# Three passes for VectorE's exp in place of five, and eighteen more score banks moved there from ScalarE

## The chip, the cores and the metric

One core of a Trainium2 chip. The metric is the device time of one execution in microseconds (us); lower is better. These kernels run on one core, so a slow state can only be told from other runs of the same kernel; all timed runs quoted here are of the state fast, and single looks (rounds 0) are of state unknown and said to be so. A ratio is taken over fast runs of the same rounds, so it is not quite the ratio of the medians quoted beside it.

## The reference

A layer normalization, 16-head attention over 2048 tokens (head size 28), and an MLP with GELU whose SiLU gates the attention's result.

```python
def _A_ref(x, wqkv, wo):                      # x: (1, 2048, 448), already normalized
    ...                                       # q, k, v: 16 heads of 28
    scores = jnp.einsum("bhqd,bhkd->bhqk", q, k) * Dh ** -0.5
    p = _softmax(scores, axis=-1)
    o = jnp.einsum("bhqk,bhkd->bhqd", p, v)
    return (...o...) @ wo

s = _A_ref(xn, A_wqkv, A_wo)
g = _silu(_B_ref(xn, B_w1, B_b1, B_w2, B_b2))  # B: GELU MLP, 448 -> 1792 -> 448
return x + s * g
```

The scores are 1024 tiles of 128 keys by 512 queries, each one PSUM bank. Every element of them needs an exp: that is the bulk of ScalarE's work.

## The kernel before

The kernel is a Python list scheduler. It holds a duration for every instruction, decides the order of each engine's instructions in advance, and emits semaphore waits for the dependencies. On the chip each engine then works down its own fixed list.

Scores are made three banks at a time (a *unit*), in a ring of six PSUM banks. ScalarE takes one exponential over the unit's banks. For some units the last bank is given to VectorE (a *late* bank), and ScalarE's exponential covers two. VectorE first evicts the bank to SBUF, which frees it, and works the exp out later, for two such banks at a time where it can.

```python
# eviction of a late bank: fixed point, the exponent's bits above bit 16
eng.tensor_scalar(K.ysb[i][...], K.ring[:, RB[m], :], SM_SCALE * LOG2E * 65536.0,
                  127.0 * 65536.0, op0=ALU.mult, op1=ALU.add)        # int32 out
...
# p_exp2: five passes over 512 or 1024 columns; lo is the low half of y as uint16
v = lo * (EXP_SC / 65536)          # tensor_scalar
u = (v + EXP_A) * v                # scalar_tensor_tensor
u = (u + EXP_B) * u                # scalar_tensor_tensor
u = v * EXP_D + u                  # scalar_tensor_tensor
pl = y * 2**-9 + u                 # scalar_tensor_tensor, written as uint16 = the bits of a bf16
```

Which units give a bank away is decided while the schedule is made: `pick_late` compares VectorE's backlog with a threshold `THS` for the block (one block is 64 banks) and with what is left of the block plus `SLACKS`. The product with V needs all of a block's late banks before the block's accumulator can be evicted. When PE's recent load is low, the scheduler also has it issue small products on zeros (L881). This is filler that changes no result.

## Time and profile before

| | before |
|---|---|
| time, median of 3 | 483.54 us (483.23 to 483.59) |
| span of the profiled run | 481.2 us |
| busy: ScalarE / PE / VectorE | 470.0 / 438.9 / 406.4 us |
| exponentials on ScalarE | 350 for 948 banks; 76 banks on VectorE |

To read it: ScalarE is the engine without gaps, so the question for each part of a change is what it does to ScalarE's list of exponentials, and whether something makes that list wait. The lines are in the prediction.

### The profile page before, as it was taken

Reading aid. Unit: us, or ns where it says so; the run is one execution under the profiler, and the core shown is the slowest. Engines: PE = TensorE matmul, PEld = TensorE weight load, DVE = VectorE, ACT = ScalarE, POOL = GpSimd, SP = SyncE. Lnnn points to the kernel's source line nnn. Section 1 sums busy time; section 2 is a strip of 40 time slices with the busy share of each in tenths; the row PEclk is TensorE's granted clock in tenths of the full one; section 3 lists DMA queues with packets and bytes.
Section 4 is the critical chain, followed back from the end, with each engine's and each line's share of the span. In section 5 each row is a group of like instructions: output and inputs, shape, how many; then the busy total and the mean of one; then the engine's idle time right before and its main releaser. Section 6 shows DMA issues by size and latency. Waiting matters only on the chain.

```text
span 481.2 us, 10207 instructions
## 1 busy us (share of the span) xinstructions
PE 438.9 (91%) x4256; PEld 169.1 (35%) x4293; DVE 406.4 (84%) x607; ACT 470.0 (98%) x394; POOL 44.7 (9%) x77
## 2 busy tenths in 40 slices
PE   6999899999988988999989988999999999899995
PEld 4443333333332333323223443333333333333453
DVE  8947789889988899999898759888897899889885
ACT  6999999999999999999999999999999999999994
POOL 7470000000000101010101000010100101000001
PEclk9999999999999999999999999999999999999998
DMA  8301000000000000000400000000101001011011
GB/s 262 136 11 26 1 1 1 1 2 2 1 1 0 1 1 1 2 2 0 135 1 0 1 2 1 0 2 1 40 0 40 2 1 38 1 59 59 3 41 40
DMA packets 8288, 11.10 MB, mean 23 GB/s; under 512 B 1649, under 2 KB 6897, under 8 KB 8242
## 3 DMA queue, kind: packets, MB, share of 16 engines
q1 hardware_dynamic: 7954, 9.75, 6.5%
q8 instruction: 34, 0.56, 0.5%
q10 hardware_dynamic: 288, 0.69, 0.4%
q14 instruction: 12, 0.10, 0.1%
HBM read 8.61 MB, written 1.84 MB: 22 GB/s over the span
## 4 chain that ended last, share of the span: by engine, by line
ACT 49%; PE 30%; issue 16%; DVE 4%; DMA 1%; POOL 0%; ACTq 0%; DVEq 0%
ACT P L1192 45%; PE ring L1153 9%; PE acc L1378 5%; PE misc L1089 4%; ACT h L1068 3%; PE misc L1031 2%; PE misc L719 2%; PE acc L881 2%; PE misc L973 1%; DVE st L629 1%; PE ring L1031 1%; DMA x_sb<-in_A_x_dram 1%; PE ring L719 1%; PE misc L1474 0%; PE ring L973 0%
## 5 line engine op out<-in xcount | busy, mean ns | idle before, releaser
L1192 ACT ACTIVATE P<-ring 128x1536 bf16<-128x1536 f32 (+1 forms) x350 | 428.8, 1501 | 0.7 <-PE ring L1153 0.5
L1153 PE MATMUL ring<-qT,kT 32*128 32x512 bf16 (+2 forms) x1144 | 136.7, 359 | 23.7 <-ACT P L1192 19.0
L1378 PE MATMUL acc<-P,vaug 128*32 128x512 bf16 (+2 forms) x1074 | 94.9, 362 | 0.5 <-issue 0.5
L1153 PEld LDWEIGHTS ring<-qT,kT 32*128 32x128 bf16 x1144 | 35.8, 91 | 130.6 <-ACT P L1192 122.2
L1215 DVE TENSOR_SCALAR x_sb<-ring 128x512 int32<-128x512 f32 x68 | 46.8, 688 | 17.7 <-PE ring L1153 16.5
L1089 PE MATMUL misc<-w,h 128*128 128x448 bf16 x224 | 51.4, 355 | 0.3
L1447 POOL CAST rhi<-rc 128x16 bf16<-128x16 f32 x15 | 11.8, 790 | 399.0 <-DVE rc L1445 296.3
L881 PE MATMUL acc<-ident,zero 128*128 128x128 bf16 x543 | 47.7, 221 | 0.2 <-issue 0.2
L1378 PEld LDWEIGHTS acc<-P,vaug 128*32 128x32 bf16 x1074 | 24.4, 93 | 51.2 <-issue 44.9
L881 PEld LDWEIGHTS acc<-ident,zero 128*128 128x128 bf16 x543 | 31.5, 98 | 21.9 <-issue 20.0
L1031 PE MATMUL misc<-xnT,w 128*128 128x512 bf16 x127 | 36.1, 382 | 1.8 <-issue 1.3
L1336 DVE SCALAR_TENSOR_TENSOR x_sb<-x_sb,kT 128x1024 uint16<-128x1024 int32 (+1 forms) x25 | 26.8, 1070 | 0.5
L1334 DVE SCALAR_TENSOR_TENSOR kT<-kT 128x1024 f32<-128x1024 f32 (+1 forms) x25 | 26.8, 1071 | 0.4
L1014 DVE CAST h<-misc 128x512 bf16<-128x512 f32 x35 | 24.0, 685 | 3.8 <-PE misc L1031 3.5
L1330 DVE SCALAR_TENSOR_TENSOR kT<-kT 128x1024 f32<-128x1024 f32 (+1 forms) x25 | 26.7, 1068 | 0.5
L1332 DVE SCALAR_TENSOR_TENSOR kT<-kT 128x1024 f32<-128x1024 f32 (+1 forms) x25 | 26.7, 1067 | 0.3
L1089 PEld LDWEIGHTS misc<-w,h 128*128 128x128 bf16 x224 | 17.7, 97 | 23.1 <-issue 10.7
L1031 PE MATMUL ring<-xnT,w 128*128 128x512 bf16 x82 | 19.4, 380 | 1.7 <-ACT h L1068 1.6
L1334 DVE SCALAR_TENSOR_TENSOR w<-w 128x1024 f32<-128x1024 f32 (+1 forms) x20 | 20.6, 1032 | 0.3
L1332 DVE SCALAR_TENSOR_TENSOR w<-w 128x1024 f32<-128x1024 f32 (+1 forms) x20 | 20.6, 1030 | 0.2
L1336 DVE SCALAR_TENSOR_TENSOR x_sb<-x_sb,w 128x1024 uint16<-128x1024 int32 (+1 forms) x20 | 20.6, 1031 | 0.2
L1330 DVE SCALAR_TENSOR_TENSOR w<-w 128x1024 f32<-128x1024 f32 (+1 forms) x20 | 20.5, 1026 | 0.3
(160 smaller groups left out, 447.4 us busy)
## 6 DMA issues: line engine op xcount, KB each, us to landing
h<-in_A_x_dram SPq DMA_DIRECT2D x4, 448.0 KB, 3.2
w<-in_B_w_dram SPq DMA_DIRECT2D x1, 1568.0 KB, 8.4
w<-in_B_w_dram SPq DMA_DIRECT2D x1, 1344.0 KB, 8.6
out_dram<-h SPq DMA_DIRECT2D x6, 224.0 KB, 1.9
x_sb<-in_A_x_dram SPq DMA_DIRECT2D x2, 448.0 KB, 4.9
h<-in_A_wqkv_dram SPq DMA_DIRECT2D x3, 168.0 KB, 5.1
x_sb<-in_A_x_dram ACTq DMA_DIRECT2D x1, 448.0 KB, 4.7
out_dram<-h SPq DMA_DIRECT2D x4, 112.0 KB, 1.7
```

The lines of the kernel that those rows point to most:

```text
L881: ins = eng.matmul(K.acc[:, 0:128], K.zero[:, :], K.ident[:, :], start=False, stop=True, skip_group_check=True)
L1014: yield _Task(DVE, lambda eng: eng.tensor_copy(dst, bank), [tok], wr, 0.69, 0.0, 2)
L1031: ins = eng.matmul(bank, K.w1[:, kt, ft * 128:(ft + 1) * 128], K.xnT[:, kt, c * 512:(c + 1) * 512], start=(kt == 0), stop=(kt == KT - 1))
L1089: ins = eng.matmul(ps, hv[:, ft, t * 128:(t + 1) * 128], K.w2[:, ft, :], start=(ft == 0), stop=(ft == FT - 1))
L1153: return eng.matmul(K.ring[:, RB[m], col:col + nq], K.kT[32 * j:32 * j + 32, g, t * 128:(t + 1) * 128], K.qT[32 * j:32 * j + 32, g, c * 51 ...
L1192: return eng.activation(K.P[:, p0:p0 + n, :], K.ring[:, b0:b0 + n, :], ACTF.Exp, scale=SM_SCALE)
L1215: yield _Task(DVE, lambda eng, m=m, i=i, half=half: eng.tensor_scalar(K.ysb[i][:, 512 * half:512 * half + 512], K.ring[:, RB[m], :], SM_SC ...
L1330: yield _Task(DVE, lambda eng: eng.scalar_tensor_tensor(u, v, EXP_A, v, op0=ALU.add, op1=ALU.mult), [tv], [tu], d1, 0.0, 4)
L1332: yield _Task(DVE, lambda eng: eng.scalar_tensor_tensor(u, u, EXP_B, u, op0=ALU.add, op1=ALU.mult), [tu], [tu], d1, 0.0, 4)
L1334: yield _Task(DVE, lambda eng: eng.scalar_tensor_tensor(u, v, EXP_D, u, op0=ALU.mult, op1=ALU.add), [tv, tu], [tu], d1, 0.0, 4)
L1336: yield _Task(DVE, lambda eng: eng.scalar_tensor_tensor(pl.bitcast(dt.uint16), y, 2.0 ** -9, u, op0=ALU.mult, op1=ALU.add), ty + [tu], [K. ...
L1378: return eng.matmul(K.acc[32 * j:32 * j + 32, q0:q0 + nq], K.vaug[:, t, 4 * g + j, :], ap[:, col:col + nq], tile_position=(0, 32 * j), sta ...
```

## The change

The intent: make VectorE's exp cheaper (three passes, not five), and use the time for 18 more banks.

The eviction now writes a float32 that stays in one binade (16384 to 32768). There its last mantissa bit is 2^-9, so its low 16 bits are the fraction of an octave, and the float itself is the bf16's bits as a number. To keep all scores in that binade, 64 octaves are added through the constant row of q; the softmax cancels them.

```diff
-THS = (8.0, 4.0, 9.0, 8.0, 4.0, 6.0, 9.0, 9.0, 8.0, 8.0, 8.0, 8.0, 8.0, 7.0, 7.0, 3.0)
-SLACKS = (6.0, 5.0, 3.0, 5.0, 0.0, 6.5, 9.0, 4.0, 3.0, 4.0, 7.0, 6.0, 8.0, 6.0, 8.0, 3.0)
+LC = 1.85
+THS = (5.0, 7.0, 15.0, 8.0, 8.0, 8.0, 8.0, 6.0, 8.0, 8.0, 8.0, 8.0, 8.0, 8.0, 8.0, 8.0)
+SLACKS = (2.0, 2.0, 6.0, 2.0, -1.0, 2.0, 2.0, 2.0, 2.0, 1.0, 2.0, 2.0, 2.0, 4.5, 2.0, 2.0)
...
-        self.plate = [... for i in range(3)]
+        self.plate = [... for i in range(3)] + [self.plx[:, 1024 * i:1024 * (i + 1)] for i in range(2)]
...
+            eng.tensor_scalar(K.coff[:, :], K.ecol[:, 0:1], 28.0, -EXP_OFF, op0=ALU.is_equal, op1=ALU.mult)
...
-                K.ysb[...], K.ring[:, RB[m], :], SM_SCALE * LOG2E * 65536.0,
-                127.0 * 65536.0, op0=ALU.mult, op1=ALU.add),
+                K.ysb[...], K.ring[:, RB[m], :], SM_SCALE * LOG2E * 128.0,
+                127.0 * 128.0, op0=ALU.mult, op1=ALU.add),
...
-        v = lo * EXP_SC / 65536          (the five passes above)
-        u = (v + EXP_A) * v
-        u = (u + EXP_B) * u
-        u = v * EXP_D + u
-        pl = y * 2**-9 + u
+        u = (lo + EXP_A) * lo
+        u = (u + EXP_B) * u
+        pl = u * EXP_K + y
```

(The passes are written as formulas here; each is one instruction.) The rest of the diff: the scheduler's thresholds use `LC`, the cost of a bank's passes; a block's finished late banks may be multiplied with V before the block's end when all output buffers are full; the eviction's other copy for eight banks at the GELU stage is changed alike.

More of the change, by code (lines that the diff above doesn't have):

```diff
@@ L52 @@
 LOG2E = 1.4426950408889634
-EXP_SC, EXP_A, EXP_B, EXP_D = 1.1449707906804418, 2.2275165815584925, 18.59640770523752, -75.73931899211772
+EXP_A, EXP_B, EXP_K = 514830.69713992253, -38047667352.91238, 3.0466089317186904e-20
+EXP_OFF = 64.0 / (LOG2E * SM_SCALE)
 LN_EPS = 1e-5
@@ L293, in alloc @@
         self.colK = sb("colK", [128, G], f32)
+        self.plx = sb("plx", [128, 2048], bf)
+        self.coff = sb("coff", [128, 1], f32)
         self.b2b = sb("b2b", [128, D], bf)
@@ L328, in alloc @@
         w2f = self.w2[:, :, :].rearrange("p f d -> p (f d)")
-        self.ysb = [xf[:, 2048 * i:2048 * (i + 1)].bitcast(dt.int32) for i in range(2)]
+        self.ysb = [xf[:, 2048 * i:2048 * (i + 1)].bitcast(f32) for i in range(2)]
         self.ylo = [xf[:, 2048 * i:2048 * (i + 1)].bitcast(dt.uint16).rearrange("p (n two) -> p n two", two=2)[:, :, 0]
                     for i in range(2)]
-        self.plate = [xf[:, 4096 + 1024 * i:5120 + 1024 * i] for i in range(3)]
-        self.ev = [w2f[:, 0:2048].bitcast(f32), self.kT[:, 0, :].bitcast(f32)]
+        self.plate = [xf[:, 4096 + 1024 * i:5120 + 1024 * i] for i in range(3)] + [self.plx[:, 1024 * i:1024 * (i + 1)] for i in range(2)]
         self.eu = [w2f[:, 2048:4096].bitcast(f32), self.kT[:, 1, :].bitcast(f32)]
@@ L336, in alloc @@
         self.b_y = [[B(), B()] for _ in range(2)]
-        self.b_pl = [B() for _ in range(3)]
-        self.b_ev, self.b_eu = [B(), B()], [B(), B()]
+        self.b_pl = [B() for _ in range(5)]
+        self.b_eu = [B(), B()]
         self.b_xn = [[B() for _ in range(4)] for _ in range(3)]
@@ L412, in schedule @@
         K.act_ms, K.p0 = [None] * NU, [0] * NU
-        K.ys, K.pls, K.pl_use = [0, 1], [0, 1, 2], [0, 0, 0]
+        K.ys, K.pls, K.pl_use = [0, 1], [0, 1, 2, 3, 4], [0] * 5
         K.ln2e = 0
@@ L538, in f @@
             eng.tensor_scalar(K.ecol[:, 2:3], K.ecol[:, 0:1], 28.0, -1.0, op0=ALU.is_equal, op1=ALU.mult)
+            eng.tensor_scalar(K.coff[:, :], K.ecol[:, 0:1], 28.0, -EXP_OFF, op0=ALU.is_equal, op1=ALU.mult)
             return eng.tensor_tensor(K.ecol[:, 3:4], K.iota_p[:, :], K.ecol[:, 0:1], ALU.subtract)
-        e(POOL, f, reads=[ec, io], writes=[K.b_cols], dur=0.8)
+        e(POOL, f, reads=[ec, io], writes=[K.b_cols], dur=1.0)
         e(POOL, lambda eng: eng.tensor_scalar(K.tcol[:, :], K.ecol[:, 3:4], 28.0, None, op0=ALU.add),
@@ L599, in late_w2 @@
             yield ("until", lambda: K.late_blk >= 2 * C)
-            for x in (K.b_ev[0], K.b_eu[0]):
-                K.b_w2.r += x.r + [x.w]
+            K.b_w2.r += K.b_eu[0].r + [K.b_eu[0].w]
             ld(K.w2[:, :, :], K.B_w2.rearrange("(ft p) d -> p ft d", p=128), K.s_w["w2"], [K.b_w2], K.now + 14)
@@ L911, in p_norm @@
         yield _Task(PE, f, [K.b_csq, K.b_bsel], [tok], 0.05, 0.15, pr)
-        yield _Task(DVE, lambda eng: eng.tensor_scalar(K.colK[:, g0:g1], bank[:, 8 + g0:8 + g1], KNORM, None,
-                                                       op0=ALU.mult), [tok], [K.b_colK], 0.17, 0.0, pr)
+        yield _Task(DVE, lambda eng: eng.tensor_scalar(K.colK[:, g0:g1], bank[:, 8 + g0:8 + g1], KNORM, K.coff[:, 0:1],
+                                                       op0=ALU.mult, op1=ALU.add), [tok, K.b_cols], [K.b_colK], 0.17, 0.0, pr)
         K.banks.append((bank, tok))
@@ L1215, in p_late @@
             yield _Task(DVE, lambda eng, m=m, i=i, half=half: eng.tensor_scalar(
-                K.ysb[i][:, 512 * half:512 * half + 512], K.ring[:, RB[m], :], SM_SCALE * LOG2E * 65536.0,
-                127.0 * 65536.0, op0=ALU.mult, op1=ALU.add),
+                K.ysb[i][:, 512 * half:512 * half + 512], K.ring[:, RB[m], :], SM_SCALE * LOG2E * 128.0,
+                127.0 * 128.0, op0=ALU.mult, op1=ALU.add),
                         [K.b_ring[RB[m]]], [K.b_y[i][half]], 0.69, 0.0, 1)
@@ L1256, in pick_late @@
                 return False
-            if K.backlog() + 3.6 > left:
+            if K.backlog() + LC + 0.69 > left:
                 K.close()
@@ L1265, in pick_late @@
             bl = K.backlog()
-            one = max(bl, 4.1) + 7.2 > left
-            if not K.ys or bl > THS[m // 64] or bl + 4.8 > left or sub > LATE_SUB:
+            one = max(bl, 4.1) + 2 * (LC + 0.69) > left
+            if not K.ys or bl > THS[m // 64] or bl + LC + 1.9 > left or sub > LATE_SUB:
                 return False
@@ L1275, in pick_late @@
         K.late_left[sub] += 1
-        K.dve_q += 3.6
+        K.dve_q += LC + 0.69
         return True
@@ L1296, in p_mlate @@
             i = K.ys.pop(0)
-            K.dve_q += 7.2
+            K.dve_q += 2 * (LC + 0.69)
             for half, m in enumerate(ms):
@@ L1306, in p_mlate @@
                 yield _Task(DVE, lambda eng, i=i, half=half, bank=bank: eng.tensor_scalar(
-                    K.ysb[i][:, 512 * half:512 * half + 512], bank, SM_SCALE * LOG2E * 65536.0,
-                    127.0 * 65536.0, op0=ALU.mult, op1=ALU.add), [tok], [K.b_y[i][half]], 0.69, 0.0, 1)
+                    K.ysb[i][:, 512 * half:512 * half + 512], bank, SM_SCALE * LOG2E * 128.0,
+                    127.0 * 128.0, op0=ALU.mult, op1=ALU.add), [tok], [K.b_y[i][half]], 0.69, 0.0, 1)
                 K.dve_q -= 0.69
@@ L1320, in p_exp2 @@
         w = 512 * len(ms)
-        v, u, y, lo, pl = K.ev[n][:, 0:w], K.eu[n][:, 0:w], K.ysb[i][:, 0:w], K.ylo[i][:, 0:w], K.plate[k][:, 0:w]
-        tv, tu, ty = K.b_ev[n], K.b_eu[n], K.b_y[i][:len(ms)]
-        d0, d1 = (0.44, 0.72) if len(ms) == 1 else (0.72, 1.14 if n == 0 else 1.24)
-        if n == 1 and tv.w is None:
+        u, y, lo, pl = K.eu[n][:, 0:w], K.ysb[i][:, 0:w], K.ylo[i][:, 0:w], K.plate[k][:, 0:w]
+        tu, ty = K.b_eu[n], K.b_y[i][:len(ms)]
+        d = 0.69 if len(ms) == 1 else 1.22
+        if n == 1 and tu.w is None:
             for c in range(C):
-                tv.r += K.b_kT[0][c].r + K.b_kT0.r
                 tu.r += K.b_kT[1][c].r
         K.late_blk = b
-        yield _Task(DVE, lambda eng: eng.tensor_scalar(v, lo, EXP_SC / 65536.0, None, op0=ALU.mult), ty, [tv], d0, 0.0, 4)
-        yield _Task(DVE, lambda eng: eng.scalar_tensor_tensor(u, v, EXP_A, v, op0=ALU.add, op1=ALU.mult),
-                    [tv], [tu], d1, 0.0, 4)
+        yield _Task(DVE, lambda eng: eng.scalar_tensor_tensor(u, lo, EXP_A, lo, op0=ALU.add, op1=ALU.mult), ty, [tu], d, 0.0, 4)
         yield _Task(DVE, lambda eng: eng.scalar_tensor_tensor(u, u, EXP_B, u, op0=ALU.add, op1=ALU.mult),
-                    [tu], [tu], d1, 0.0, 4)
-        yield _Task(DVE, lambda eng: eng.scalar_tensor_tensor(u, v, EXP_D, u, op0=ALU.mult, op1=ALU.add),
-                    [tv, tu], [tu], d1, 0.0, 4)
-        yield _Task(DVE, lambda eng: eng.scalar_tensor_tensor(pl.bitcast(dt.uint16), y, 2.0 ** -9, u,
-                                                              op0=ALU.mult, op1=ALU.add),
-                    ty + [tu], [K.b_pl[k]], d1, 0.0, 4)
-        K.dve_q -= 2.91 * len(ms)
+                    [tu], [tu], d, 0.0, 4)
+        yield _Task(DVE, lambda eng: eng.scalar_tensor_tensor(pl.bitcast(dt.uint16), u, EXP_K, y, op0=ALU.mult, op1=ALU.add),
+                    ty + [tu], [K.b_pl[k]], d, 0.0, 4)
+        K.dve_q -= LC * len(ms)
         K.ln2e = 0
@@ L1354, in p_pv @@
             b = first
-            yield ("until", lambda: K.exp_m >= ms[-1] and K.E_done >= first - 1 and (
-                not end or len([x for x in K.late_ready if K.sub_of(x[0]) == b]) == K.late_left[b]))
+            mine = lambda: [x for x in K.late_ready if K.sub_of(x[0]) == b]
+            yield ("until", lambda: K.exp_m >= ms[-1] and K.E_done >= first - 1)
+            while end and len(mine()) < K.late_left[b]:
+                yield ("until", lambda: len(mine()) == K.late_left[b] or (not K.pls and len(mine()) > 0))
+                if len(mine()) < K.late_left[b]:
+                    yield from self.pv_task(q, mine()[:4], [])
             late = []
@@ L1361, in p_pv @@
                     late.append((m, k, half))
-            for x in late:
-                K.late_ready.remove(x)
-            K.late_left[b] -= len(late)
-            src = [(m, K.P[:, K.PB[m], :], K.b_P[K.PB[m]]) for m in ms if m not in K.late]
-            src += [(m, K.plate[k][:, 512 * half:512 * half + 512], K.b_pl[k]) for m, k, half in late]
-            src = sorted(src[:4], key=lambda x: x[0] % 4) + src[4:]
-            fl, rd = [], []
-            for kk in range(4):
-                for m, ap, tok in src:
-                    _, j, pc, _, s = K.pieces(m)
-                    g = q // 16 // C
-                    if kk >= len(pc):
-                        continue
-                    t, q0, nq, col = pc[kk]
-                    def f(eng, t=t, j=j, g=g, q0=q0, nq=nq, col=col, ap=ap):
-                        return eng.matmul(K.acc[32 * j:32 * j + 32, q0:q0 + nq], K.vaug[:, t, 4 * g + j, :],
-                                          ap[:, col:col + nq], tile_position=(0, 32 * j), start=(t == 0),
-                                          stop=(t == T - 1), skip_group_check=True)
-                    fl.append(f)
-                    rd += [tok, K.b_v[0 if g == 0 else 1][t]]
-            def fall(eng, fl=fl):
-                ins = None
-                for f in fl:
-                    ins = f(eng)
-                return ins
-            yield _Task(PE, fall, rd, [K.b_acc], 0.36 if len(src) < 5 else 0.6, 0.1,
-                        lambda: 1.2 if K.exp_u - K.pv_u > 4 or K.exp_u > NU - 4 or GU - 1 <= K.exp_u <= GU else 6)
+            yield from self.pv_task(q, late, ms)
             for m in ms:
                 K.pv_done[m] = True
-            for _, k, _ in late:
-                K.pl_use[k] -= 1
-                if K.pl_use[k] == 0:
-                    K.pls.append(k)
             K.pv_u = UOF[ms[-1]]
@@ L1399, in p_pv, with pv_task, f, fall @@
                 K.spawn(K.p_epi(b) if b < NBLK - 1 else K.p_epi4(first - NBLK + 1), 0.5)
+    def pv_task(self, q, late, ms):
+        K = self
+        b = K.sub_of((late[0][0] if late else ms[0]))
+        for x in late:
+            K.late_ready.remove(x)
+        K.late_left[b] -= len(late)
+        src = [(m, K.P[:, K.PB[m], :], K.b_P[K.PB[m]]) for m in ms if m not in K.late]
+        src += [(m, K.plate[k][:, 512 * half:512 * half + 512], K.b_pl[k]) for m, k, half in late]
+        src = sorted(src[:4], key=lambda x: x[0] % 4) + src[4:]
+        fl, rd = [], []
+        for kk in range(4):
+            for m, ap, tok in src:
+                _, j, pc, _, s = K.pieces(m)
+                g = q // 16 // C
+                if kk >= len(pc):
+                    continue
+                t, q0, nq, col = pc[kk]
+                def f(eng, t=t, j=j, g=g, q0=q0, nq=nq, col=col, ap=ap):
+                    return eng.matmul(K.acc[32 * j:32 * j + 32, q0:q0 + nq], K.vaug[:, t, 4 * g + j, :],
+                                      ap[:, col:col + nq], tile_position=(0, 32 * j), start=(t == 0),
+                                      stop=(t == T - 1), skip_group_check=True)
+                fl.append(f)
+                rd += [tok, K.b_v[0 if g == 0 else 1][t]]
+        def fall(eng, fl=fl):
+            ins = None
+            for f in fl:
+                ins = f(eng)
+            return ins
+        yield _Task(PE, fall, rd, [K.b_acc], 0.36 if len(src) < 5 else 0.6, 0.1,
+                    lambda: 1.2 if K.exp_u - K.pv_u > 4 or K.exp_u > NU - 4 or GU - 1 <= K.exp_u <= GU else 6)
+        for _, k, _ in late:
+            K.pl_use[k] -= 1
+            if K.pl_use[k] == 0:
+                K.pls.append(k)
     def sub_of(self, m):
```

## The prediction

> **What bounds the kernel now.** I read the page first: its shares of busy time, then its row for ScalarE in the 40 slices.
>
> ```profile
> PE 438.9 (91%) x4256; PEld 169.1 (35%) x4293; DVE 406.4 (84%) x607; ACT 470.0 (98%) x394; POOL 44.7 (9%) x77
> ACT  6999999999999999999999999999999999999994
> ...
> L1192 ACT ACTIVATE P<-ring 128x1536 bf16<-128x1536 f32 (+1 forms) x350 | 428.8, 1501 | 0.7 <-PE ring L1153 0.5
> ```
>
> ScalarE is busy from the second slice to the last but one. 428.8 us of it is one line, the softmax exponential: 350 instructions over three PSUM banks of 512 columns each, or over two where VectorE takes the third (or at the start, where units hold two). The table of windows, cut before the first of these exponentials and after the last, agrees:
>
> ```profile
> 0.00:12.60 12.60, 8.34 (x68) 5.87 (x69) 10.64 (x40) 8.32 (x23) 9.40 (x28) 1.00 0.84 257
> 12.60:474.00 461.40, 428.13 (x4165) 162.32 (x4200) 391.31 (x560) 460.65 (x372) 33.24 (x47) 1.00 0.05 16
> 474.00:481.20 7.20, 2.48 (x28) 0.95 (x25) 4.47 (x9) 1.06 (x3) 2.06 (x2) 0.79 0.16 50
> ```
>
> (After the window and its length: busy time of PE, weight loads, DVE, ACT, POOL, then clock and DMA.) In 461.4 us ScalarE rests 0.75 us. VectorE has 70 us free there. PE's 428 us contain 47.7 us of filler on zeros (L881, issued to keep its clock up), so it has room as well. Head (12.6 us) and tail (7.2 us) are other chains.
>
> The busy share hides one thing. In the timeline of ScalarE, cut so fine that each exponential has its own row (start, duration), starts are a better clock than durations:
>
> ```profile
> 207.51 1.29 ACT L1192 ACTIVATE P<-ring 128x1024 bf16<-128x1024 f32 x1
> 208.69 1.04 ACT L1192 ACTIVATE P<-ring 128x1024 bf16<-128x1024 f32 x1
> ...
> 212.27 1.06 ACT L1192 ACTIVATE P<-ring 128x1024 bf16<-128x1024 f32 x1
> 213.17 1.50 ACT L1192 ACTIVATE P<-ring 128x1536 bf16<-128x1536 f32 x1
> 214.50 1.51 ACT L1192 ACTIVATE P<-ring 128x1536 bf16<-128x1536 f32 x1
> ```
>
> From start to start, the two-bank exponential at 212.27 takes 0.90 us and the three-bank one after it 1.33 us. These are the shortest pitches anywhere in the trace (0.903 and 1.330), and nearly all of the 249 three-bank ones have 1.330. The one at 207.51 has 1.18: ScalarE waited some 0.27 us for the next scores, and no gap shows since its record (1.29 us) runs past that start. Summing pitch less shortest pitch over the trace gives 1.3 us for the 32 two-bank units at the start, 0.7 us for all three-bank ones and **3.7 us for the 68 units whose third bank VectorE took**, 0.054 us each. So unloading a bank costs a little of what it gains. At the stalls, the scores come late mostly as PE was inside another task when the bank came free.
>
> **What the Trainium skill says.** (1) "ScalarE: Activation LUTs", section "What ACT_TABLE_LOAD costs": an ACTIVATE handles one element per cycle and lane at 1.2 GHz, whatever the function; 512 columns are 427 ns. The trace agrees: 1.330 - 0.903 = 0.427. (2) "Perfetto Trace Analysis", section "DVE / Act Engine Instruction": a record runs from the start in the ALUs to the acknowledged write. That fits overlapping records here (mean 1,501 ns, but 428.8/350 = 1,225 ns apart). (3) "VectorE: DVE Perf Modes", section "The TRN2 errata": a two-tensor fp32 operation takes (N+151)/0.96 ns, 1,224 ns for 1024 elements; in section "The perf-mode tier table" two-tensor fp32 stays at one element per cycle. The trace has 1,206 to 1,219 ns for the two-tensor operation used here, and 681 ns for the one-source pass.
>
> **The change part by part.** VectorE's exp of a pair of banks is now one eviction of 512 columns per bank and five passes over 1024, in this order (the listing by line and form; mean ns after the busy time):
>
> ```profile
> L1215 DVE TENSOR_SCALAR x_sb<-ring 128x512 int32<-128x512 f32 x68 | 46.8, 688 | 17.7 <-PE ring L1153 16.5
> ...
> L1334 DVE SCALAR_TENSOR_TENSOR kT<-kT 128x1024 f32<-128x1024 f32 x18 | 21.9, 1219 | 0.2
> L1336 DVE SCALAR_TENSOR_TENSOR x_sb<-x_sb,kT 128x1024 uint16<-128x1024 int32 x18 | 21.9, 1219 | 0.3
> L1330 DVE SCALAR_TENSOR_TENSOR kT<-kT 128x1024 f32<-128x1024 f32 x18 | 21.9, 1215 | 0.3
> L1332 DVE SCALAR_TENSOR_TENSOR kT<-kT 128x1024 f32<-128x1024 f32 x18 | 21.8, 1213 | 0.1
> ...
> L1329 DVE TENSOR_SCALAR kT<-x_sb 128x1024 f32<-128x1024 uint16 x18 | 12.3, 681 | 0.4
> ```
>
> Before, a pair costs 2 x 0.69 + 0.68 + 4 x 1.216 = 6.92 us, 3.46 a bank. A lone bank costs 0.69 + 0.415 + 4 x 0.69 = 3.87. There are 31 pairs and 14 lone ones: 31 x 6.92 + 14 x 3.87 = 269 us, which the rows of the eight groups add up to.
>
> *Removed:* the pass that turns the fraction into float32 (0.68) and one of the four two-tensor passes (1.22). A float32 in one binade has the fraction in its low 16 bits already, so the quartic's first factor reads those directly as both operands, the second works in place, and the last adds to the float itself. All three have two tensors at 4-byte stride or width, so I give each 1.22 us at 1024 and 0.69 at 512, as now: no faster mode. A pair then costs 1.38 + 3 x 1.22 = 5.04, a lone bank 2.76. If four fifths of the banks go in pairs as now, 94 banks cost about 94 x 2.57 = 241 us. **VectorE gives back 28 us although it takes 18 more banks**, to some 378 us busy. It is not the bound, so this alone is worth nothing; it is what lets it take the 18.
>
> *Moved:* 18 banks leave ScalarE. The number of exponentials stays 350, for a unit of three becomes one of two: 18 x (1.330 - 0.903) = **7.7 us less** in the stretch that is saturated. All of it is on the path that sets the end.
>
> *Given back:* 18 more such units at 0.054 us of hidden wait: 18 x 0.054 = **1.0 us**. The schedule (thresholds of backlog, slack to the block's end) is set anew, and I can only take the present rate.
>
> *Added elsewhere:* one GpSimd operation of some 0.24 us among the constants (its neighbours at L537 and L538 take 0.23 and 0.24). GpSimd's weight square then ends near 8.0 instead of 7.73 us, while PE reads it only at 8.60: hidden, or at most 0.1 us. Two more output buffers for finished banks, five for three, and the flush of finished banks before a block's end make VectorE wait less for the PV product; they add no matmul for any bank. The tail is not touched.
>
> Sum: -7.7 + 1.0 + 0.1 = -6.6 us on 483.54: **476.9**, rounded down to **476.8** as less work on VectorE may mend a little of the stalls.
>
> **The rivals.** *A: ScalarE gets all of it.* VectorE's queue is shorter, evictions come sooner, and the stall stays 3.7 us or falls: 474.8 to 475.9. For it: 28 us freed on VectorE. Against: in the stalls that I looked at, PE's own order was late more often than the eviction, and VectorE's longest instruction stays 1.22 us. *B: the stall grows with density.* 86 units in place of 68 lie closer together, often two in a row, and a two-bank exponential leaves PE 0.9 us for scores and whatever task it began. PE has the same work in less time. The worst pair of rows now has 0.37 and 0.39 us, where two such units follow each other (312.3 and 313.6 us). At 0.10 us each, 86 give 8.6 us, 4.9 more than now: 480.7. Against: the new settings were presumably chosen by the time they gave. *C: VectorE's finished banks hold up the block's end.* A block's accumulator is released only after its last late bank; slack figures of mostly 2 in place of mostly 3 to 9 say that the queue is made to finish earlier, so I expect under 1 us: 477 to 478. *D: the first pass, reading a 16-bit stream at stride two twice, is slower than 1.22.* At double time it adds some 60 us to VectorE, which would then be full, and banks would come late: over 485. The one-source pass on that very stream takes 681 ns, the fast rate, so I give it 2%.
>
> **Range and chances.** A sets the low side, B half-way the high side: 475.0 to 479.2. Faster by over 2% needs under 473.9, more than the 7.7 us plus 1.9 of the stalls: 0.04. Slower by over 2% needs D and more: 0.01. Within 2%: 0.95.
>
> **What would show it.** ScalarE's exponential line: still 350, busy 421 to 423 in place of 428.8, 231 of three banks at 1.33 us apart and 118 of two; banks on ScalarE 930. VectorE: three passes, each 1.2 us at 1024, busy 370 to 385. Span about 474.5; head within 0.2 us of 12.6, tail the same 7. The hidden wait at units of two banks 4 to 5.5 us. I am wrong if that wait is under 2 or over 8 us, if ScalarE shows open gaps in mid-span, or if the first pass takes other than 1.2 us.

## The result, and the profile after

476.32 us median of 4 runs (475.78 to 477.04), against 483.56 (4 runs) for the kernel before: ratio 0.9854, interval 0.984 to 0.9868. The predicted 476.8 is 0.5 us off and the range holds it. The runs fall in two groups, near 475.8 and near 476.9; the second has a granted clock of 0.994 or 0.995 in place of 0.998 to 1.0. The profiled run is of the first.

The page after, its busy shares and its costliest group:

```profile
PE 435.4 (92%) x4150; PEld 164.0 (35%) x4185; DVE 379.2 (80%) x550; ACT 462.4 (98%) x394; POOL 39.7 (8%) x78
...
L1195 ACT ACTIVATE P<-ring 128x1536 bf16<-128x1536 f32 (+1 forms) x350 | 420.5, 1467 | 0.6 <-PE ring L1156 0.3
```

VectorE has 27 us less to do although it handles 94 banks; ScalarE's exponentials are still 350 but 8.3 us shorter in all. The table of windows, cut at nearly the same points of the program (PE, weight loads, DVE, ACT, POOL, clock, DMA after the window and its length):

```profile
0.00:12.60 12.60, 7.94 (x66) 5.46 (x66) 10.88 (x39) 8.16 (x21) 9.31 (x29) 1.00 0.87 263
12.60:467.00 454.40, 425.11 (x4064) 157.64 (x4096) 364.89 (x505) 453.40 (x374) 28.30 (x48) 1.00 0.05 16
467.00:474.00 7.00, 2.31 (x25) 0.89 (x25) 3.47 (x7) 0.84 (x2) 2.06 (x2) 1.00 0.15 49
```

Nearly all of the gain is in the middle stretch, which is 7.0 us shorter and still saturated (ScalarE rests 1.0 us of 454.4). The passes, by line and form (mean ns after the busy time):

```profile
L1331 DVE SCALAR_TENSOR_TENSOR kT<-x_sb 128x1024 f32<-128x1024 uint16 x24 | 29.2, 1217 | 0.5
L1332 DVE SCALAR_TENSOR_TENSOR kT<-kT 128x1024 f32<-128x1024 f32 x24 | 29.1, 1212 | 0.2
...
L1334 DVE SCALAR_TENSOR_TENSOR x_sb<-kT,x_sb 128x1024 uint16<-128x1024 f32 x15 | 18.3, 1221 | 0.2
```

The 16-bit stream read twice costs what two float32 tensors cost.

To account for the span I summed ScalarE's pitches from start to start, as in the prediction: the *work* is each exponential at its shortest pitch (1.330 us for three banks, 0.903 for two), the *hidden wait* is what a pitch has beyond it.

| part of the span, us | before | after | difference |
|---|---|---|---|
| to the first exponential | 12.60 | 12.84 | +0.24 |
| exponentials, at shortest pitch | 421.47 | 413.78 | -7.69 |
| hidden wait, 32 units at the start | 1.33 | 1.33 | 0 |
| hidden wait, three-bank units | 0.32 | 0.36 | +0.04 |
| hidden wait, units with a late bank (68, 86) | 3.70 | 3.28 | -0.42 |
| wait between an exponential and a GELU or tanh | 0.38 | 0.61 | +0.23 |
| GELU, tanh, table loads and the one exponential over a single bank, with their waits | 33.75 | 34.21 | +0.46 |
| after the last exponential's shortest pitch, to the end | 7.66 | 7.57 | -0.09 |
| span | 481.21 | 473.99 | -7.22 |

The rows add up to the spans within rounding. The work term is as predicted; the hidden wait did not grow by 1 us but fell by 0.4.

### The profile page after: what moved, and what is told of

Same layout as the page of the kernel before. It is cut to its first block, busy times and chain, and to the rows that moved or that the text cites. A ratio compares the mean times of both kernels' runs of the same rounds, so it can differ in the third digit from the quotient of the medians.

```text
span 474.0 us, 9973 instructions
## 1 busy us (share of the span) xinstructions
PE 435.4 (92%) x4150; PEld 164.0 (35%) x4185; DVE 379.2 (80%) x550; ACT 462.4 (98%) x394; POOL 39.7 (8%) x78
## 4 chain that ended last, share of the span: by engine, by line
ACT 43%; PE 38%; issue 13%; DVE 4%; DMA 1%; ACTq 0%; DVEq 0%
ACT P L1195 41%; PE ring L1156 11%; PE acc L1389 7%; PE misc L1092 5%; PE misc L1034 4%; PE acc L884 2%; PE misc L722 2%; ACT h L1071 2%; PE ring L1034 2%; PE misc L1480 1%; PE misc L976 1%; DMA x_sb<-in_A_x_dram 1%; PE ring L722 1%; PE ring L976 1%; DVE kT L1331 0%
## 5 line engine op out<-in xcount | busy, mean ns | idle before, releaser
L1195 ACT ACTIVATE P<-ring 128x1536 bf16<-128x1536 f32 (+1 forms) x350 | 420.5, 1467 | 0.6 <-PE ring L1156 0.3
L1156 PE MATMUL ring<-qT,kT 32*128 32x512 bf16 (+2 forms) x1144 | 136.4, 359 | 22.0 <-ACT P L1195 16.3
L1218 DVE TENSOR_SCALAR x_sb<-ring 128x512 f32<-128x512 f32 x86 | 59.2, 688 | 26.8 <-PE ring L1156 25.9
L1156 PEld LDWEIGHTS ring<-qT,kT 32*128 32x128 bf16 x1144 | 35.6, 91 | 130.0 <-ACT P L1195 119.7
L884 PE MATMUL acc<-ident,zero 128*128 128x128 bf16 x435 | 40.4, 221 | 0.0
L1034 PE MATMUL misc<-xnT,w 128*128 128x512 bf16 x128 | 36.2, 382 | 1.4 <-issue 0.8
L1017 DVE CAST h<-misc 128x512 bf16<-128x512 f32 x35 | 24.1, 688 | 10.8 <-PE misc L1034 10.6
L1331 DVE SCALAR_TENSOR_TENSOR kT<-x_sb 128x1024 f32<-128x1024 uint16 (+1 forms) x28 | 32.0, 1141 | 0.7
L884 PEld LDWEIGHTS acc<-ident,zero 128*128 128x128 bf16 x435 | 25.1, 97 | 20.5 <-issue 19.0
L1332 DVE SCALAR_TENSOR_TENSOR kT<-kT 128x1024 f32<-128x1024 f32 (+1 forms) x28 | 31.9, 1138 | 0.4
L1331 DVE SCALAR_TENSOR_TENSOR w<-x_sb 128x1024 f32<-128x1024 uint16 (+1 forms) x22 | 25.7, 1168 | 0.4
L1332 DVE SCALAR_TENSOR_TENSOR w<-w 128x1024 f32<-128x1024 f32 (+1 forms) x22 | 25.8, 1171 | 0.2
L1034 PE MATMUL ring<-xnT,w 128*128 128x512 bf16 x82 | 19.7, 380 | 0.8 <-ACT h L1071 0.6
L1334 DVE SCALAR_TENSOR_TENSOR x_sb<-kT,x_sb 128x1024 uint16<-128x1024 f32 (+1 forms) x16 | 19.0, 1187 | 0.2
L1071 ACT ACTIVATE h<-h 128x2560 bf16<-128x2560 bf16 (+2 forms) x8 | 16.6, 2073 | 0.0
L733 DVE TENSOR_SCALAR kT<-misc,ecol 128x512 bf16<-128x512 f32 x13 | 9.7, 748 | 8.3 <-PE misc L722 8.1
L1334 DVE SCALAR_TENSOR_TENSOR x_sb<-w,x_sb 128x1024 uint16<-128x1024 f32 (+1 forms) x14 | 16.0, 1142 | 0.1
```

What stands on the lines that cost most here:

```text
L884: ins = eng.matmul(K.acc[:, 0:128], K.zero[:, :], K.ident[:, :], start=False, stop=True, skip_group_check=True)
L1017: yield _Task(DVE, lambda eng: eng.tensor_copy(dst, bank), [tok], wr, 0.69, 0.0, 2)
L1034: ins = eng.matmul(bank, K.w1[:, kt, ft * 128:(ft + 1) * 128], K.xnT[:, kt, c * 512:(c + 1) * 512], start=(kt == 0), stop=(kt == KT - 1))
L1071: yield _Task(ACT, lambda eng, dst=dst, src=src: eng.activation(dst, src, ACTF.Gelu_apprx_tanh), rd, K.b_hf[c][f0:f0 + n] + ([K.b_h[c]] if ...
L1156: return eng.matmul(K.ring[:, RB[m], col:col + nq], K.kT[32 * j:32 * j + 32, g, t * 128:(t + 1) * 128], K.qT[32 * j:32 * j + 32, g, c * 51 ...
L1195: return eng.activation(K.P[:, p0:p0 + n, :], K.ring[:, b0:b0 + n, :], ACTF.Exp, scale=SM_SCALE)
```

## The experiments

The questions: is the gain the count of banks on ScalarE and nothing else; what does VectorE's freed time count for; where does the hidden wait come from; and why 94 banks, not more. In what follows, "the changed kernel" as a control ran again on the same chip as the first four: 475.9 us median (475.81 to 477.01, 4 runs), hidden wait at late units 3.16 us.

> The changed kernel once more, as the control of the runs beside it on the same chip. 475.8 to 477.0 us as before; the exponential line on ScalarE busy 420.5 us, hidden wait at two-bank units 3.3 us. If its runs again fall in two groups about 1.1 us apart, the control's spread is what smaller effects have to be held against.

So runs of the changed kernel again lie in two groups 1.1 us apart (three near 475.9, one at 477.01), and effects under about 0.5 us can't be read from times.

**One part alone: the arithmetic.** The old 76 positions are listed, and `pick_late` reads the list.

```diff
+FIXED = [[33, 36], [44, 47], [54, 57], [58, 61], [66], ...]   # the units and pairs of the kernel before
+        if u not in ROLE: return False        # ROLE: unit -> place in its pair
```

> The new arithmetic, but the old kernel's 76 banks at the old units and in the old pairs. Theory (only the count of banks on ScalarE matters): ScalarE's exponential line is back at 427.5 to 429.5 us busy and the time at 483 to 484.5, although VectorE's busy time falls from 406 by some 74 us to about 332 (31 pairs at 5.04 and 14 lone banks at 2.76 in place of 6.92 and 3.87). Rival (a shorter queue on VectorE is worth something by itself, through less hidden wait and an earlier block end): 480 to 482, with the hidden wait of the 68 two-bank units down from 3.7 to under 2.5 us.

Measured: 483.7 us (483.54 to 483.98, 5 runs), ratio to before 1.0004 (0.9991 to 1.0018). VectorE's busy time fell to 340.4 us (I had said 332), the exponential line is 428.3 us, the hidden wait at the 68 late units 3.73 us against 3.70. The page's two lines:

```profile
PE 446.7 (93%) x4299; PEld 168.5 (35%) x4299; DVE 340.4 (71%) x517; ACT 470.2 (98%) x394; POOL 42.6 (9%) x78
...
L1199 ACT ACTIVATE P<-ring 128x1536 bf16<-128x1536 f32 (+1 forms) x350 | 428.3, 1484 | 0.8 <-PE ring L1158 0.5
```

**Freeing 66 us on VectorE alone is worth nothing**; the rival falls. This run also has the new buffers and the flush.

**The other part alone: the banks.** The old five passes at the changed kernel's 94 positions, with the new buffers (the diff is the old eviction and passes back in, and the list of the 94).

> The old five passes at the changed kernel's 94 banks, same units and pairs, with the new buffers and flush. VectorE's need is 379 + 44 x 1.88 + 6 x 1.11 = 468 us in a span of 474, and in most blocks more than the block lasts. Theory (the cheaper exp is what makes the 94 possible): VectorE busy about 468, ScalarE with many open gaps, and far over 483; the scheduler's own end is 530.8, so 515 to 535. Rival (the old kernel's settings simply left banks unused, and the old arithmetic would do at 94): 476 to 480.

528.79 us. ScalarE's open waits, longest first (in total, times, longest):

```profile
ACT P L1202 <- PE ring L1161: 38.5, 28, 6.0
ACT P L1202 <- PE acc L1384: 7.5, 8, 1.6
```

VectorE is 464.2 us busy. So the two parts are worth nothing or harm each alone, and the gain needs both. That the old kernel merely left banks unused is out. A second form of the same question let the scheduler choose for the old passes, in the changed kernel's buffers; a search over its thresholds found 77 banks at most.

```diff
+LC = 2.91
+THS = (5.0, 3.0, 7.0, 6.0, 8.0, ...)         # and SLACKS, from a search for the scheduler's earliest end
```

> The old arithmetic of five passes inside the changed kernel (its five output buffers, its flush before a block's end), with thresholds set anew by the same scheduler and search: it finds 77 banks at most, end 482.2 us. Theory (the passes decide how many banks fit; buffers and flush give little by themselves): 482 to 484 us. Rival (buffers and flush are a good part of the gain): under 480.

Measured: 485.79 us (485.21 to 486.24, 4 runs), ratio 1.0048. That is above my 482 to 484: three-bank units waited 3.1 us, and the first exponential came at 13.74 us. But nothing speaks for the rival, that buffers and flush give a good part of the gain: they are in this run and in the one with the arithmetic alone, and neither gained.

**More work on VectorE, order unchanged.** My prediction called VectorE's 70 idle microseconds free. Here a useless pass is put in before the first, with zero duration told to the scheduler, so that every engine's order stays the changed kernel's.

```diff
+        yield _Task(DVE, lambda eng: eng.tensor_scalar(u, lo, 1.0 / 65536.0, None, op0=ALU.mult), ty, [tu], 0.0, -0.03, 4)
         yield _Task(DVE, lambda eng: eng.scalar_tensor_tensor(u, lo, EXP_A, lo, op0=ALU.add, op1=ALU.mult), ty, [tu], d, 0.0, 4)
```

> The changed kernel with one useless pass put back per pair or lone bank (the 16-bit stream to float32, 0.68 us at 1024, 0.415 at 512: 44 x 0.68 + 6 x 0.415 = 32 us more on VectorE), with the order of every engine's instructions otherwise the same. VectorE busy 411 us, more than in the kernel before. Theory (VectorE has slack, and the hidden wait comes from PE's order): within 1 us of the changed kernel, hidden wait at the 86 two-bank units 2.8 to 4 us. Rival (the hidden wait fell short of my prediction of 4.7 us because VectorE's queue is shorter): hidden wait back to 4.5 us or more, and time up by 1.2 us or more.

Measured: 488.45 us (488.39 to 488.68, 4 runs), 12.6 us more than the control. **My theory fell**: VectorE was busy 408.6 us, as in the kernel before, and yet the time is 5 us worse than before. The hidden wait at late units rose to 8.47 us, at three-bank units to 6.62, and the wait for the MLP's first product at the GELU to 2.0. ScalarE now has open gaps too (those before exponentials are inside these sums), of which the waits show:

```profile
ACT P L1195 <- PE ring L1156: 5.6, 19, 1.1
```

The longest of them, in the timeline of this run (start, duration, in brackets the idle time before and what ended it; L733 evicts a K projection from the bank `misc`, L722 makes the next one there, L1156 makes scores):

```profile
56.45 1.23 DVE L1332 SCALAR_TENSOR_TENSOR w<-x_sb 128x1024 f32<-128x1024 uint16 x1
...
57.59 0.75 DVE L733 TENSOR_SCALAR kT<-misc,ecol 128x512 bf16<-128x512 f32 x1
58.25 0.68 DVE L1218 TENSOR_SCALAR x_sb<-ring 128x512 f32<-128x512 f32 x1
58.39 0.55 PEld L722 LDWEIGHTS misc<-xnT,wk 128*128 128x128 bf16 x4 [1.20 <-DVE kT L733]
...
59.36 0.10 PEld L1156 LDWEIGHTS ring<-qT,kT 32*128 32x128 bf16 x3 [0.42 <-issue]
...
59.80 1.45 ACT L1195 ACTIVATE P<-ring 128x1536 bf16<-128x1536 f32 x1 [1.07 <-PE ring L1156]
```

The same place in the changed kernel:

```profile
55.92 0.75 DVE L733 TENSOR_SCALAR kT<-misc,ecol 128x512 bf16<-128x512 f32 x1
...
56.95 0.55 PEld L722 LDWEIGHTS misc<-xnT,wk 128*128 128x128 bf16 x4 [0.23 <-DVE kT L733]
57.92 0.10 PEld L1156 LDWEIGHTS ring<-qT,kT 32*128 32x128 bf16 x3 [0.42 <-ACT P L1195]
```

In both, VectorE's eviction L733 stands behind a pass. With the spare pass it comes late, PE waits 1.20 us at the head of its list for the bank `misc`, and the scores, which have nothing to do with that bank, stand behind it in the list. Here VectorE reached ScalarE through PE's fixed order; the other waits of this run were not followed up one by one.

**Less work on VectorE, order unchanged.** The middle pass is cut to one column but keeps its duration in the scheduler (the quartic is then wrong).

```diff
-        yield _Task(DVE, lambda eng: eng.scalar_tensor_tensor(u, u, EXP_B, u, op0=ALU.add, op1=ALU.mult),
+        yield _Task(DVE, lambda eng: eng.scalar_tensor_tensor(u[:, 0:1], u[:, 0:1], EXP_B, u[:, 0:1], op0=ALU.add, op1=ALU.mult),
```

> The changed kernel with its middle pass cut to one column (the result is wrong on purpose), the plan not told and so every engine's order the same. VectorE some 50 us less busy, about 327 us. Theory (with the plan met, VectorE's earliness is of no use, as the waits that are left come from PE's order and ScalarE's releases): 475.4 to 477 us, hidden wait at the 86 two-bank units 2.6 to 3.7 us. Rival (the same chain through VectorE that cost 12 us when it was longer gives time back when it is shorter): under 475, hidden wait under 2 us.

Measured: 475.84 us (475.67 to 476.37, 4 runs), ratio 0.9847. VectorE's busy time is 331.7 us, 47.5 less than in the changed kernel, and the exponential line is the changed kernel's to the last digit:

```profile
L1195 ACT ACTIVATE P<-ring 128x1536 bf16<-128x1536 f32 (+1 forms) x350 | 420.5, 1467 | 0.6 <-PE ring L1156 0.3
```

The hidden wait at late units is 3.28 us in both, and the same units wait. The unit at 175.03 in the changed kernel (its wait is 1.22 - 0.903 = 0.32 us) against the one at 175.35 here, each exponential in its own row; first the changed kernel, then this one:

```profile
175.03 1.40 ACT L1195 ACTIVATE P<-ring 128x1024 bf16<-128x1024 f32 x1
176.25 1.53 ACT L1195 ACTIVATE P<-ring 128x1536 bf16<-128x1536 f32 x1
```

```profile
175.35 1.40 ACT L1195 ACTIVATE P<-ring 128x1024 bf16<-128x1024 f32 x1
176.57 1.53 ACT L1195 ACTIVATE P<-ring 128x1536 bf16<-128x1536 f32 x1
```

So at the exponentials VectorE's effect is one-sided: late costs, early is not used. What hidden wait is left there does not come through this pass. One wait did go: 0.35 us before a GELU at 266.09 us in the changed kernel, for the MLP's first product, is not in this run. The row of GELU and tanh falls from 34.21 to 33.84 us; the head is 0.32 us longer in this profile, so the spans are alike.

**More work on VectorE, order made for it.** The spare pass again, its duration told, and the thresholds searched anew for 94 banks.

```diff
+        yield _Task(DVE, lambda eng: eng.tensor_scalar(u, lo, ...), ty, [tu], 0.44 if len(ms) == 1 else 0.72, 0.0, 4)
-LATE_GAP, LATE_SUB = 3, 15
+LATE_GAP, LATE_SUB = 2, 15
+LC = 2.21                                     # and new THS, SLACKS
```

> The useless fourth pass again, and again 94 banks on VectorE, but now the plan is told of the pass: its thresholds were set anew by the kernel's own list scheduler, whose figure for the end is 474.8 us (it gave 475.6 for the changed kernel, 482.5 for the one before). VectorE busy about 410 us, as in the run with the spare pass that the plan did not know. Theory (that run lost 12 us because instructions ran later than the fixed order of PE's queue assumes, not because VectorE was full): 475 to 478 us, hidden wait at two-bank units under 5 us, and no open gap over 0.5 us on ScalarE in mid-span. Rival (VectorE at 410 us with 94 banks is itself the bound): 482 us or more.

Measured: 478.55 us (478.26 to 478.73, 4 runs), ratio 0.9901. VectorE is busy 409.7 us, as with the unplanned pass, and 9.9 of the 12.6 us are gone. So a plan that knows of the pass avoids most of that loss, which fits my theory. The search also chose other units and pairs, and the run was on another chip than the control, so order and choice are not told apart. 2.65 us against the control are left, a little over the 478 that I allowed: hidden wait 5.32 us at late units (I had said under 5) and 1.69 at three-bank ones. Whether a better search would remove them, or VectorE's load does cost that much, these runs do not tell.

**More banks.** Thresholds from a search over the changed kernel's own settings.

```diff
+THS = (5.0, 4.0, 9.0, 5.0, 7.0, 8.0, 5.0, 4.0, 5.0, 7.0, 5.0, 8.0, 5.0, 9.0, 7.0, 12.0)
+SLACKS = (2.0, 5.0, 3.0, 3.0, 2.0, 5.0, 0.0, 1.5, 1.5, 7.0, 7.0, 7.0, 7.0, 7.0, 2.5, 2.5)
```

> The changed kernel with thresholds found by its own list scheduler: 103 banks on VectorE, not 94; the scheduler's end is 471.6 against 475.6 us. Theory (the count of banks on ScalarE decides while the plan is met): 9 x 0.427 = 3.8 us less work, some 0.5 us more hidden wait, so 472.3 to 473.8 us; VectorE busy 379 + 9 x 2.55 = 402. Rival (94 was where VectorE or PE begins to hold ScalarE up): 475 us or more, with hidden wait over 6 us.

Measured: **472.07 us** (471.99 to 472.21, 4 runs), ratio 0.9768 (0.9753 to 0.9782): better than both kernels, and just under the 472.3 to 473.8 that I expected. The work at shortest pitch is 409.94 us, 3.84 less than in the changed kernel, and the hidden wait at the now 95 late units 3.58 us. VectorE is busy 400.1 us, nearly what it was in the kernel before:

```profile
PE 431.7 (92%) x4134; PEld 163.2 (35%) x4170; DVE 400.1 (85%) x580; ACT 458.6 (98%) x394; POOL 43.4 (9%) x78
...
L1195 ACT ACTIVATE P<-ring 128x1536 bf16<-128x1536 f32 (+1 forms) x350 | 417.1, 1413 | 0.8 <-PE ring L1156 0.5
```

The rival, that 94 was the limit, falls.

**Too many banks.** Loose thresholds, 15 and 6 us in every block.

> The changed kernel with loose thresholds (15 and 6 us in every block): 106 banks go to VectorE, three more than in the best plan, but up to the end of each block. If only the count mattered, ScalarE would have 12 x 0.427 = 5.1 us less to do than in the changed kernel and the time would be about 471. The kernel's own scheduler puts the end at 493.9. Theory (a plan that lets VectorE's backlog reach over a block's end makes PE, and so ScalarE, wait there): 485 to 496 us, with open gaps on ScalarE of several us in all. Rival (count alone): under 474.

492.1 us, within what I expected, but not by the mechanism I named. The block ends cost little: the hidden wait at late units is 4.24 us and the exponential line 415.4 us, shorter than the 417.1 with 103 banks. The loss is nearly all one wait:

```profile
ACT h L1071 <- PE ring L1034: 20.0, 1, 20.0
```

L1071 is the GELU, L1034 the MLP's first product. ScalarE stands still from 263.8 to 283.8 us. Here is what PE and VectorE do in the second part of it:

```profile
272.42 0.55 PEld L1034 LDWEIGHTS misc<-xnT,w 128*128 128x128 bf16 x4 [0.29 <-DVE h L1017]
...
273.50 0.69 DVE L1017 CAST h<-misc 128x512 bf16<-128x512 f32 x1
...
274.24 0.55 PEld L1034 LDWEIGHTS misc<-xnT,w 128*128 128x128 bf16 x4 [0.29 <-DVE h L1017]
...
275.32 0.69 DVE L1017 CAST h<-misc 128x512 bf16<-128x512 f32 x1
```

Product and eviction take turns on the one spare bank `misc`, 1.82 us for each tile: the first-layer products that PE makes between the scores were not done when the GELU was due. VectorE had evicted 28 of the 35 tiles (L1017) by the GELU's start, against all 35 in the kernel with 103 banks. In the first part of the stall, up to 272 us, VectorE is busy 7.99 of 8.20 us, mostly with exps of banks that it was given. Why the seven tiles were late is not shown. It was not for lack of PE's time: from the first exponential to the GELU, PE spent 27.6 us on filler (L884), against 20.2 with 103 banks. VectorE had 55 late banks there against 49, and was busy 212.1 of 241.9 us against 204.5 of 243.7. Nothing in the thresholds watches this side work.

**The head.** The first exponential starts 0.24 us later in the changed kernel's profile. Two tries at the cause: the new GpSimd constant moved behind the weight square (all orders the same), and, in the kernel of 103 banks, the old order of PE's work in the head (scheduler told 0.8 for 1.0 us).

```diff
+            yield K.wsquare(POOL, 0, 1, 0.85)
+            yield _Task(POOL, lambda eng: eng.tensor_scalar(K.coff[:, :], K.ecol[:, 2:3], EXP_OFF, None, op0=ALU.mult), ...)
```

> The changed kernel with the new GpSimd constant made after the weight square instead of before it, all orders else the same. Theory (the 0.24 us by which the first exponential starts later than in the kernel before, 12.84 against 12.60 us, come from this operation): the first exponential starts at 12.5 to 12.7 us. Rival (they come from another order of PE's work in the head, or from when the input landed): it stays at 12.8 to 12.9. The time itself should move by 0.2 us at most, which these runs can't resolve.

```diff
-        e(POOL, f, reads=[ec, io], writes=[K.b_cols], dur=1.0)
+        e(POOL, f, reads=[ec, io], writes=[K.b_cols], dur=0.8)
```

> The kernel with 103 banks at the same units, with the scheduler told 0.8 instead of 1.0 us for the GpSimd constants, so that PE's order in the head is the old kernel's again (the new GpSimd operation stays). Moving that operation did not bring the first exponential back. Theory (PE's order in the head costs the 0.25 us): the first exponential starts 8.5 to 8.7 us after ScalarE's first read of x, as in the kernel before (8.59), against 8.8 to 9.0 in the changed kernels. Rival (what is left of the operation on GpSimd, or chance): 8.8 or more. Time 471.5 to 472.3 us; 0.25 us is at the edge of what these runs tell apart.

Measured: 476.48 us (476.06 to 476.95, 4 runs) with the first exponential at 13.13 us, and 472.1 us (471.99 to 472.29, 5 runs) with it at 13.15, 9.18 us after ScalarE's first read of x. **Neither theory is borne out.** The first run is no clean test: in it the weight square waited for a weight DMA, to 7.17 us (it started at 6.80 in the kernel before). Over the profiles of all changed versions the first exponential lies between 12.84 and 13.74 us, so 0.24 us is within what one profile to the next differs by (12.84 and 12.96 for the changed kernel itself). Counted from ScalarE's first read of x they take 8.8 to 9.8 us, against 8.59 in the one profile of the kernel before; so a true delay is not excluded, and the cause stays open.

## Why the prediction was right

*The bound.* Right: the middle stretch decides, and it became shorter by the work taken from ScalarE.

*Moved, 7.7 us.* Right in mechanism and size: 7.69 us by the pitches, and 3.84 more for nine more banks. With the arithmetic alone there is no gain (1.0004), which is the step "this alone is worth nothing".

*The cost of the new exp.* Right: 1.21 to 1.22 us a pass at 1024, VectorE 379.2 us busy against "some 378". Of the other signs, ScalarE's line came out at 420.5 us, just under the 421 to 423 named, and the hidden wait at 3.28, under the 4 to 5.5 named.

*Given back, 1.0 us.* Wrong in sign: the hidden wait at late units fell by 0.4 us. The step that failed is "I can only take the present rate", 0.054 us a unit. The rate belongs to a plan, not to a unit: 0.054 before, 0.055 with the new arithmetic at the old positions, 0.038 with the 94, again 0.038 with the 103, and 0.062 with the told fourth pass. What in a plan sets it is not shown. The remark that less work on VectorE may mend some of it was wrong as a reason: with 47.5 us less on VectorE the same units wait the same 3.28 us. Rival A's low stall thus came true, but not for its reason.

*Added elsewhere, 0.1 us.* 0.24 us in this profile at the head, not settled; and 0.7 us around the GELU stage (0.23 + 0.46 in the table), which I had not counted. The latter is not in the kernel with 103 banks (0.50 us of wait and 33.74 us), so it too belongs to a plan. The sum is -7.69 + 0.24 + 0.69 + 0.04 - 0.42 - 0.09 = -7.23 us of span, against -6.6 predicted. The stall came out 1.4 us better than said and these smaller parts 0.8 us worse. That the number is only some 0.5 us off is thus in part luck.

*"VectorE has 70 us free there."* True as an idle time, wrong as a reserve: 29 us more cost 12.6 us when the order did not know of them. Rival D had the right kind of harm (banks late because a pass is longer), and I gave it a threshold of +60 us; with the order unchanged, half that hurt.

*Rival B*, growth of the stall with density, did not happen at 94 or 103 banks. At 106 the loose plan did harm, but in the MLP's first products and not in the stalls. *Rival C* left no sign: the listed waits of ScalarE in the changed kernel name no wait of an exponential for the accumulator.

*The range.* Its high side, 479.2, is called half-way to rival B; half of B's 4.9 us gives 478.3 (483.54 - 7.7 + 2.45) and the mean of 476.8 and 480.7 gives 478.75. So the range was a little wide; the measured 476.3 lies inside the narrower one too.

## What to carry to other kernels

When the bound engine is saturated, an offload is worth the work it takes away, read as start-to-start pitch and not as busy time; freeing the engine that receives it is worth nothing until it is used. Idle time of an engine in a fixed order is no reserve: ask which in-order list waits for it, and re-make the plan with true durations whenever an instruction's cost changes. When more work is moved to VectorE, check the side work that must be done by a given stage, here the MLP's first products before the GELU.

## What the Trainium skill lacked or had wrong

- "Perfetto Trace Analysis", section "Identifying the Most-Contended Engine", takes occupancy as a fair measure of how close ScalarE is to its limit. Here occupancy is 98% in the kernel before and an idle time of 0.7 us stands at the exponentials, while the pitches show 5.4 us of waits within them (1.33 + 0.32 + 3.70); records that overlap hide them.
- "ScalarE: Activation LUTs", section "What ACT_TABLE_LOAD costs", gives 186 ns + 0.833 N for an ACTIVATE with immediates and about 93 ns of overlap, without saying which memory it reads; that would be, as an estimate, 1,373 and 946 ns from start to start at 1536 and 1024 columns. The exponentials, reading PSUM, show 1,330 and 903, so a fixed 50 ns. "Perfetto Trace Analysis", section "Optimizing Scalar/DVE Operations", has about 51 ns for PSUM, and the runs agree with that one.
- The records' overlap is no fixed 93 ns here (same section of "ScalarE: Activation LUTs"): in the rows at 175.03 and 176.25 it is 1.40 - 1.22 = 0.18 us, and in the prediction's first rows 0.11 us, between neighbours of one kernel.
- No page has the cost of a two-tensor operation with a scalar that reads a 16-bit stream at stride two: 1,217 ns at 1024 columns, the rate of two float32 tensors.
- No page warns that an idle engine's slack is not free under a fixed order: 29 us of added work on VectorE, which idled some 95 us of the span, cost 12.6 us.
